# A routed expert chosen from 24 of 32 slots: 19 weight buffers, slot sums in two tiles, the expert's load moved

## The chip, the core and the metric

The kernel runs on one core of a Trainium2 chip. The metric is the device time of one execution in microseconds (us); runs are given as a median with the lowest and highest. The engines are TensorE (PE; PEld is its weight load), VectorE (DVE), ScalarE (ACT), GpSimd (POOL) and SyncE (SP, whose queue issues nearly all transfers here).

## The reference

Three parts follow each other: attention with a bias from relative positions, a soft mixture of experts with 8 experts of 4 slots, and a routed layer in which each token goes to one of 8 experts.

```python
# attention -> x [2304, 512]
logits = x @ phi                                  # [2304, 32 slots]
d = softmax over tokens of logits;  slot_input = d.T @ x
for e in range(8):                                # 4 slots per expert
    h = np.maximum(slot_input[e] @ w1[e], 0.0)    # w1[e] [512, 1024]
    slot_out[e] = h @ w2[e]                       # w2[e] [1024, 512]
c = softmax over slots of logits
x = c @ slot_out
# routed layer
do_compute = x @ w_skip > 0
e_idx = argmax(x @ w_gate)                        # one of 8 experts per token
h = np.maximum(x[mask] @ gw1[e], 0.0)
out = x + gate_w * (h @ gw2[e])                   # tokens without do_compute: out = x
```

## The kernel before

Attention takes the first 340 us. Then come the slots' experts. Their weights, 32 MB, are streamed in 64 pieces of 512 KB: pieces 0 to 31 are the first matrices (four per expert), pieces 32 to 63 the second. `weight_piece` (L228) takes the next buffer and issues the load on SP. The list `SLOTS` (L220) holds 3 + 10 + NW2 buffers: three that are used once, ten that the attention has left (sq, sk, k, bias), and NW2 = 12 new ones (`x0` to `x11`), 25 in all. From piece 25 on a piece reuses the buffer of the piece 22 before it, and its load waits for that piece's matmuls; the last 22 buffers form the ring. The loops over pieces issue one more load after each piece's matmuls.

The first loop (L895 to L902) multiplies pieces 0 to 31 with the slot inputs into `ph`; the second (L975 to L983) multiplies pieces 32 to 63 with the hidden values `hT` into the PSUM tile `pbig`. Between them stand a softmax over slots and its transposes (L909, L869; VectorE's scaling of it is L932), and the transposes of the hidden values (L950). The last piece is loaded in two halves (L243).

After the second loop `pbig` is copied by halves (L985, L986), summed over four row groups with a matmul against `sel` (L989), copied to `ST4` (the 32 slot outputs, transposed; L992, L993) and multiplied with the gate and skip vectors (L996, `pw`), which gives `SW`, the scores of each slot (L1000, L1001). The expert for the routed layer is guessed: a matmul with ones (L1099) sums the scores over the 32 slots, `max` and `max_index` (L1100, L1101) and a clamp (L1102) give an index, SP loads it into a register (L1103) and issues the expert's 4 MB as eight loads of 512 KB (`expert_load`, L1019: four of `w1e`, four of `w2e`). The two tiles lie in the pool `gw`, in memory that the weight buffers had.

Behind that, TensorE runs 19 routing matmuls (L1114), four transposes of `ST4` (L1117), then `slots(0)` with the first quarter of `w1e` (L1034), a counting matmul (L1127) that needs VectorE's `cnt` (L1123), `slots(1)`, `slots_sum(0)` (L1042), and so on in an order written out by hand. `x2` (L1056) forms the output of the slot layer. The list of experts that tokens really chose is compared with the guess (L1219 to L1221): if there is one and it is the guess, a short branch (L1266 to L1283) finishes and stores; otherwise the general branch (L1284) loads each chosen expert again and runs all its matmuls, 24 of 512 columns for each of 18 token tiles.

The order of instructions on each engine comes from a planner that simulates the program, except inside `manual_schedule`, where the order of the source holds: the attention follows the due times of `SCHED` and `LAST`, and everything from L1000 to the stores follows the source. `issue_after(ins)` ties instructions behind one of the same engine. In the two weight loops and between them the planner orders.

```python
def weight_piece():
    i = len(wq)
    name, shape, dt = SLOTS[i] if i < len(SLOTS) else SLOTS[NW + (i - NW) % (len(SLOTS) - NW)]
...
for i in range(32):
    ...
    pe.matmul(po[g * 32:(g + 1) * 32, :], lhsT=hT[:, o:o + NSL], rhs=wq[32 + i][:, a * 512:(a + 1) * 512], start=(i < 2), stop=(i >= 30))
    if len(wq) < 64:
        weight_piece()
...
pe.matmul(pe_g[:, 0:10], lhsT=onesr, rhs=SW, start=True, stop=True)
vec.max(out=g8, in_=pe_g[:, 0:8])
vec.max_index(out=g8i, in_max=g8, in_values=pe_g[:, 0:8])
expert_load(sync.value_load(g_i[0:1, 0:1], min_val=0, max_val=7))
```

Of the kernel before, what the change touches and what calls it, by code (L numbers as in the profile page):

```python
# [9 lines left out]
F32 = mybir.dt.float32  # L10
# [10 lines left out]
P = 128  # L21
# [75 lines left out]
NW2 = 12  # L97
# [8 lines left out]
def soft_moe_attention_kernel(ctx, tc, q, k, v, w1, b1, w2, phi, mw1, mw2,  # L106
# [111 lines left out]
    wq = []  # L218
# [9 lines left out]
    def weight_piece():  # L228
# [593 lines left out]

    for i in range(NW2):
        wpools[f"x{i}"] = wctx.enter_context(tc.tile_pool(name=f"wx{i}", bufs=1, side="right", reuse_waits="tile"))
# [31 lines left out]
    with ExitStack() as mctx:  # L856
# [106 lines left out]
        onesr = late.tile([P, P], F32R, name="onesr")  # L963
# [6 lines left out]
        vec.tensor_copy(onesr, ones)  # L970
# [13 lines left out]
        part = late.tile([P, DM], F32, name="part")  # L984
        act.copy(part[:, 0:256], po[:, 0:256])  # L985
        vec.tensor_copy(part[:, 256:512], po[:, 256:512])  # L986
        pt = [ps.tile([P, 512], F32, name="pc") for _ in range(2)]
        for kc in range(4):
            pe.matmul(pt[kc // 2][:, kc % 2 * P:(kc % 2 + 1) * P], lhsT=part[:, kc * P:(kc + 1) * P], rhs=sel,  # L989
                      start=True, stop=True)  # L990
# [20 lines left out]
    w1e = gw.tile([P, 4, FF], F32, name="w1e")  # L1011
    w2e = gw.tile([P, 8, DM], F32, name="w2e")
# [5 lines left out]

    def expert_load(ereg):  # L1019
        for a in range(4):  # L1020
            f = slice(a * 256, (a + 1) * 256)
            sync.dma_start(out=w1e[:, :, f], in_=gw1[bass.ds(ereg, 1), :, f].rearrange("o (k p) f -> p (o k) f", p=P))
        for a in range(4):
            f = slice(a * 256, (a + 1) * 256)
            sync.dma_start(out=w2e[:, 2 * a:2 * a + 2, :],
                           in_=gw2[bass.ds(ereg, 1), f, :].rearrange("o (k p) f -> p (o k) f", p=P))
# [33 lines left out]
    with tc.tile_pool(name="gq", bufs=1, reuse_waits="tile") as gq:  # L1060
# [33 lines left out]
        g8 = gq.tile([P, 8], F32, name="g8")  # L1094
        g8i = gq.tile([P, 8], mybir.dt.uint32, name="g8i")
# [5 lines left out]
        vec.max_index(out=g8i, in_max=g8, in_values=pe_g[:, 0:8])  # L1101
        vec.tensor_scalar(out=g_i, in0=g8i[:, 0:1], scalar1=7.0, scalar2=0.0, op0=ALU.min, op1=ALU.max)  # L1102
        expert_load(sync.value_load(g_i[0:1, 0:1], min_val=0, max_val=7))  # L1103
        vec.tensor_scalar(out=goff[:, 0:1], in0=g_i, scalar1=8.0, scalar2=None, op0=ALU.subtract)
        vec.tensor_scalar(out=goff[:, 1:2], in0=g_i, scalar1=float(FF), scalar2=None, op0=ALU.mult)
# [10 lines left out]
        for kc in range(4):  # L1116
            pe.transpose(p4[:, kc * P:(kc + 1) * P], ST4[:, kc, :], ident)  # L1117
# [261 lines left out]
```

## Time and profile before

| | us |
|---|---|
| median of 3 runs | 492.16 |
| lowest, highest | 491.25, 494.73 |
| the profiled execution | 491.48 |
| span of its profile | 489.6 |
| PE, DVE, ACT busy | 420.0, 354.4, 301.7 |

The profile shows one execution. Times in its rows count from the start of the span. Busy shares of the whole span mix stages with different limits, so the stretch around the change is read by itself.

### The profile page before, as it was taken

The page shows a single profiled execution, that of the slowest core. Times are in us where ns is not written, and L with a number is a line of the kernel's source. Part 1 is how long each engine was busy: PE and PEld are TensorE (multiplying, and loading weights), DVE is VectorE, ACT ScalarE, POOL GpSimd, SP SyncE. Part 2 cuts the span into 40 slices and gives each one's busy share as a digit, 9 for nine tenths or more (in the row PEclk, how much of TensorE's full clock was granted, in tenths as well). Part 3 has the DMA queues.
Part 4 walks back from the last instruction along what each step waited for, and adds up shares of the span by engine and source line. Part 5 has one row for each costly group of instructions (what it writes and reads, how often), then busy time and mean ns, then how long its engine had stood idle before and what let it go on. Part 6 is the DMA issues. An engine that isn't in the chain of part 4 may idle for free.

```text
span 489.6 us, 11571 instructions
## 1 busy us (share of the span) xinstructions
PE 420.0 (86%) x4291; PEld 302.8 (62%) x4291; DVE 354.4 (72%) x824; ACT 301.7 (62%) x633; POOL 252.6 (52%) x243
## 2 busy tenths in 40 slices
PE   4786997988998989889988999998797777799983
PEld 2442466877888879879967988886363111255462
DVE  6998977976978989878988898996648100047563
ACT  4887978796886888859968879892402100027510
POOL 5630027998887899869997899772300000000000
PEclk9989998998998999989999999999989799959998
DMA  6458864999899999899999989799999999572065
GB/s 184 163 173 306 296 245 88 219 196 234 176 206 210 198 231 187 205 231 197 228 201 245 213 198 175 172 194 215 410 386 407 387 387 387 197 253 93 27 214 177
DMA packets 154076, 111.49 MB, mean 228 GB/s; under 512 B 120256, under 2 KB 126912, under 8 KB 154016
## 3 DMA queue, kind: packets, MB, share of 16 engines
q1 hardware_dynamic: 152112, 107.47, 84.8%
q10 hardware_dynamic: 1824, 2.97, 1.8%
q8 instruction: 36, 0.59, 0.5%
q0 software_dynamic: 80, 0.26, 0.2%
q14 instruction: 24, 0.20, 0.1%
HBM read 66.97 MB, written 15.34 MB: 168 GB/s over the span
## 4 chain that ended last, share of the span: by engine, by line
PE 33%; DMA 33%; DVE 16%; ACT 8%; issue 5%; POOL 3%; SPq 1%; ACTq 0%; DVEq 0%; POOLq 0%
DMA eT<-ehl 9%; PE sc L452 7%; DVE ehl L491 7%; DMA x<-in_moe_w_dram 7%; DMA bias<-in_moe_w_dram 4%; DMA scratch<-ev 4%; DVE e L469 3%; ACT ev L211 3%; PE av L589 3%; PE av L581 2%; PE sc L208 2%; PE ph L899 2%; DMA tn<-in_v_dram 2%; DMA k<-in_moe_w_dram 2%; DMA bias<-scratch 2%
## 5 line engine op out<-in xcount | busy, mean ns | idle before, releaser
L469 DVE CUSTOM_DVE_ANT_0 e<-sc,bias 128x576 f32<-128x576 f32 x128 | 95.0, 753 | 26.9 <-PE sc L452 21.2
L452 PE MATMUL sc<-k,qT 128*128 128x288 f32 x512 | 100.6, 324 | 6.0 <-DVE st L469 4.5
L476 ACT ACTIVATE e<-e,st 128x576 f32<-128x576 f32 x128 | 96.3, 778 | 4.2 <-DVE st L469 3.6
L491 DVE SCALAR_TENSOR_TENSOR ehl<-e,ehl 128x1152 f16<-128x1152 f32 x48 | 83.8, 1746 | 0.5 <-POOL ehl L487 0.4
L452 PEld LDWEIGHTS sc<-k,qT 128*128 128x128 f32 x512 | 74.8, 195 | 11.5 <-DVE st L469 7.4
L487 POOL TENSOR_SCALAR ehl<-e 128x1152 f16<-128x1152 f32 x48 | 60.2, 1262 | 7.9 <-ACT e L476 4.5
L208 PE MATMUL sc<-hid,w2b 128*32 128x288 f32 x576 | 49.9, 433 | 10.7 <-ACT ev L211 7.8
L204 DVE TENSOR_SCALAR hid<-ll,nib 128x576 f32<-128x576 f32 x117 | 55.7, 557 | 2.8 <-PE sc L208 2.8
L395 POOL TENSOR_TENSOR v<-tv,v 128x650 f16<-128x650 f32 x16 | 31.0, 1936 | 44.6 <-ACT v L391 44.6
L424 POOL TENSOR_SCALAR k<-k 64x1152 fp32r<-64x1152 f32 x30 | 51.5, 1717 | 4.6 <-ACT k L414 1.4
L581 PE MATMUL av<-v,eT 128*128 128x65 f16 x1152 | 51.3, 195 | 0.0
L208 PEld LDWEIGHTS sc<-hid,w2b 128*32 128x32 f32 x576 | 23.2, 114 | 35.2 <-ACT ev L211 20.7
L581 PEld LDWEIGHTS <-eT 128*128 128x128 f16 x1152 | 43.8, 99 | 0.9
L1106 POOL TENSOR_SCALAR Lt<-rk 128x128 f16<-128x128 f32 x1 | 0.3, 299 | 75.9 <-PE pbig L980 75.9
L211 ACT ACTIVATE ev<-sc,offs,ipi 128x576 f32<-128x576 f32 x36 | 29.9, 829 | 9.2 <-PE sc L208 5.6
L986 DVE COPY part<-pbig 128x256 f32<-128x256 f32 x1 | 0.4, 425 | 41.7 <-ACT part L985 41.7
L589 PE MATMUL av<-eq,tv 128*64 128x192 f32 x320 | 29.5, 331 | 0.0
L374 POOL TENSOR_SCALAR sk<-tk 128x576 fp32r<-128x576 f32 x16 | 18.1, 1131 | 21.8 <-DMA tk<-in_k_dram 14.5
L376 POOL TENSOR_TENSOR sq<-tq,sq 128x576 fp32r<-128x576 f32 x16 | 27.0, 1690 | 1.1
L985 ACT COPY part<-pbig 128x256 f32<-128x256 f32 x1 | 0.4, 373 | 42.6 <-PE pbig L980 42.6
L544 PE MATMUL pt<-ident,e 128*128 128x128 f32 x144 | 24.8, 285 | 0.5 <-ACT eq L549 0.5
L980 PE MATMUL pbig<-x,hT 128*32 128x512 f32 x76 | 20.5, 623 | 4.8 <-DMA x<-in_moe_w_dram 4.8
(335 smaller groups left out, 881.2 us busy)
## 6 DMA issues: line engine op xcount, KB each, us to landing
x<-in_moe_w_dram SPq DMA_DIRECT2D x30, 512.0 KB, 10.7
scratch<-ev SPq DMA_DIRECT2D x36, 288.0 KB, 4.6
bias<-scratch SPq DMA_DIRECT2D x16, 576.0 KB, 4.7
tn<-in_v_dram SPq DMA_DIRECT2D x32, 224.0 KB, 3.8
bias<-in_moe_w_dram SPq DMA_DIRECT2D x13, 512.0 KB, 10.2
k<-in_moe_w_dram SPq DMA_DIRECT2D x12, 512.0 KB
tk<-in_k_dram SPq DMA_DIRECT2D x16, 288.0 KB, 3.9
tq<-in_q_dram SPq DMA_DIRECT2D x16, 288.0 KB, 4.1
```

The source lines that it names most:

```text
L204: vec.tensor_scalar(out=hid, in0=src, scalar1=nib[:, gi:gi + 1], scalar2=None, op0=ALU.max)
L208: pe.matmul(pb[c * 32:(c + 1) * 32, hh, 0:288], lhsT=w2b, rhs=hid[:, hh * 288:(hh + 1) * 288], start=True, stop=True)
L211: act.activation(ev, pb[:, :, 0:288].rearrange("p a (l u) -> p u a l", u=NU), AF.Identity, bias=offs[not on_act], scale=ipi[:, bt:bt + 1])
L395: pool.tensor_tensor(out=z["v16"][:, 1], in0=tv, in1=z["v16"][:, 0], op=ALU.subtract)
L424: pool.tensor_scalar(out=k1[64 * i:64 * i + 64], in0=k0[64 - 64 * i:128 - 64 * i], scalar1=1.0, scalar2=1.0, op0=ALU.mult, op1=ALU.mult)
L452: pe.matmul(sc[:, hh, 0:288], lhsT=l_, rhs=kf[i][:, o:o + 288], start=(i == 0), stop=(i == 1))
L469: vec.tensor_tensor_reduce(out=z["e", t][:, o].rearrange("p (a j) -> p a j", a=2), in0=z.pop(("sc", t, j))[:, :, 0:288], in1=bias_t[hp, t] ...
L476: act.activation(ee, ee, AF.Exp, bias=z["m", t][:, j:j + 1], scale=-1.0, **kw)
L487: pool.tensor_scalar(out=eh[:, 0], in0=z["e", t], scalar1=ES, scalar2=1.0, op0=ALU.mult, op1=ALU.mult)
L491: vec.scalar_tensor_tensor(out=eh[:, 1], in0=z.pop(("e", t)), scalar=ES, in1=eh[:, 0], op0=ALU.mult, op1=ALU.subtract)
L581: pe.matmul(av[:, oj:oj + VD], lhsT=eT[:, ei, 5 * j + c], rhs=v16[:, vi, c, j], start=False, stop=lastt and k_ == 2 and c == 3)
L589: pe.matmul(z["av", 1][j * 64:(j + 1) * 64, o], lhsT=tv[:, c, j, 0:64], rhs=z["eq"][:, 4 * j + c if c < 4 else 8], start=False, stop=last ...
```

## The change

The ring of weight buffers shrinks (NW2 from 12 to 6: 19 buffers, the last 16 form the ring). The expert's tiles `w1e` and `w2e` get a pool of their own that is open before the weight loops. The second loop writes slots 0 to 23 (pieces 32 to 55) and slots 24 to 31 (pieces 56 to 63) into two PSUM tiles. After piece 55 the first tile is copied, summed over all its rows with ones, multiplied with the gate, and the index of the greatest score becomes the guess; the expert's loads are tied behind the last weight piece on SP. The first tile's part of the slot sums (`to_T(0)`) is done there too, the second tile's after the loop. The guess after `SW` goes, and the four transposes of `ST4` stand ahead of the 19 routing matmuls.

```diff
-NW2 = 12
+NW2 = 6
...
-                eng.dma_start(out=t2[:, a], in_=src[:, a])
+                last_piece[:] = [eng.dma_start(out=t2[:, a], in_=src[:, a])]
...
+    ew = ctx.enter_context(tc.tile_pool(name="ew", bufs=1, side="right", reuse_waits="tile"))
+    w1e = ew.tile([P, 4, FF], F32, name="w1e")
+    w2e = ew.tile([P, 8, DM], F32, name="w2e")
...
-        vec.tensor_copy(onesr, ones)
...
-        po = p1.tile([P, DM], F32, name="pbig", bufs=2)
+        po = [p1.tile([P, DM], F32, name="pbig", bufs=2) for _ in range(2)]
+        part = [late.tile([P, DM], F32, name=f"part{i}") for i in range(2)]
+        pt = [ps.tile([P, 512], F32, name="pc") for _ in range(2)]
+        GE = 24
+        def half_sums(i):
+            act.copy(part[i][:, 0:256], po[i][:, 0:256])
+            vec.tensor_copy(part[i][:, 256:512], po[i][:, 256:512])
+        def to_T(i):
+            for kc in range(4):
+                pe.matmul(pt[kc // 2][:, kc % 2 * P:(kc % 2 + 1) * P], lhsT=part[i][:, kc * P:(kc + 1) * P], rhs=sel,
+                          start=i == 0 and kc % 2 == 0, stop=i == 1 and kc % 2 == 1)
+        def guess_a():
+            half_sums(0)
+            pgs = p1.tile([P, 512], F32, name="pgs")
+            for kc in range(4):
+                pe.matmul(pgs[:, kc * P:(kc + 1) * P], lhsT=part[0][:, kc * P:(kc + 1) * P], rhs=ones,
+                          start=True, stop=True)
+            gsum = sp.tile([P, 512], F32, name="gsum")
+            act.copy(gsum[:, 0:256], pgs[:, 0:256])
+            vec.tensor_copy(gsum[:, 256:512], pgs[:, 256:512])
+            pe_g = p1.tile([P, 10], F32, name="pwg")
+            for kc in range(4):
+                pe.matmul(pe_g, lhsT=gsum[:, kc * P:(kc + 1) * P], rhs=w10[:, kc, :], start=kc == 0, stop=kc == 3)
+            vec.max(out=g8, in_=pe_g[:, 0:8])
+            vec.max_index(out=g8i, in_max=g8, in_values=pe_g[:, 0:8])
+            vec.tensor_scalar(out=g_i, in0=g8i[:, 0:1], scalar1=7.0, scalar2=0.0, op0=ALU.min, op1=ALU.max)
+            with tc.issue_after(last_piece[0].ins):
+                expert_load(sync.value_load(g_i[0:1, 0:1], min_val=0, max_val=7))
...
+            to_T(0)
...
-                pe.matmul(po[g * 32:(g + 1) * 32, :], lhsT=hT[:, o:o + NSL],
-                          rhs=wq[32 + i][:, a * 512:(a + 1) * 512], start=(i < 2), stop=(i >= 30))
+                pe.matmul(po[i // GE][g * 32:(g + 1) * 32, :], lhsT=hT[:, o:o + NSL],
+                          rhs=wq[32 + i][:, a * 512:(a + 1) * 512], start=i % GE < 2, stop=i in (GE - 2, GE - 1, 30, 31))
             if len(wq) < 64:
                 weight_piece()
+            if i == GE - 1:
+                guess_a()
+        half_sums(1)
+        to_T(1)
...
-        pe_g = pg.tile([P, 512], F32, name="pc")
-        pe.matmul(pe_g[:, 0:10], lhsT=onesr, rhs=SW, start=True, stop=True)
-        vec.max(out=g8, in_=pe_g[:, 0:8])
...
-        expert_load(sync.value_load(g_i[0:1, 0:1], min_val=0, max_val=7))
...
+        p4 = pg.tile([P, 512], F32, name="pc")
+        for kc in range(4):
+            pe.transpose(p4[:, kc * P:(kc + 1) * P], ST4[:, kc, :], ident)
         pl = py.tile([P, 512], F32, name="y")[:, 0:NA * 10].rearrange("p (t x) -> p t x", x=10)
         for t in range(NA):
             pe.matmul(pl[:, t, :], lhsT=cT(t) if t < NT else cO, rhs=SW, start=True, stop=True)
-        p4 = pg.tile([P, 512], F32, name="pc")
-        for kc in range(4):
-            pe.transpose(p4[:, kc * P:(kc + 1) * P], ST4[:, kc, :], ident)
```

## Rows read from the trace of the kernel before

**Rows 1.** The page: DMA's busy share in 40 slices, in tenths.
```profile
DMA  6458864999899999899999989799999999572065
```
**Rows 2.** The chain that ended last, 410 us on: start, us, what.
```profile
411.80 10.75 DMA x<-in_moe_w_dram
422.59 2.36 PE pbig L980 x8
...
431.03 4.84 DMA w1e<-in_moe_w_dram
436.00 1.08 PE pc L1034 x8
...
449.96 1.00 PE y L1207 x8
```
**Rows 3.** Timeline, 428 to 437: start, us, engine, line, operation, [idle before <- releaser].
```profile
428.45 1.85 PE L1114 MATMUL y<-SW,bias 128*128 128x10 f32 x8
...
432.29 0.35 PE L1114 MATMUL y<-SW,cO 128*128 128x10 f32 x1
...
432.50 1.11 PE L1117 MATMUL pc<-ident,bias 128*128 128x128 f32 x4
...
433.73 0.42 DVE L1123 TENSOR_REDUCE cnt<-ea 128x8 f32<-128x144 f32 x1
433.92 0.20 PEld L1034 LDWEIGHTS pc<-w1e,bias 128*32 128x32 f32 x8 [0.70 <-DMA w1e<-in_moe_w_dram]
...
434.93 0.60 PE L1127 MATMUL y<-cnt,ones 128*128 128x8 f32 x2
...
436.00 1.08 PE L1034 MATMUL pc<-w1e,bias 128*32 128x256 f32 x8 [0.47 <-DMA w1e<-in_moe_w_dram]
```
**Rows 4.** Stretches: length, five engines' busy us (instructions), granted clock, DMA share, GB/s.
```profile
428.00:429.00 1.00, 0.69 (x4) 0.72 (x4) 0.50 (x4) 0.00 (x0) 0.00 (x0) 0.69 0.00 0
...
431.00:432.00 1.00, 1.00 (x6) 1.00 (x6) 0.00 (x0) 0.00 (x0) 0.00 (x0) 0.50 0.27 52
...
441.00:442.00 1.00, 1.00 (x9) 0.23 (x2) 0.55 (x1) 0.23 (x2) 0.00 (x0) 0.50 1.07 393
442.00:443.00 1.00, 1.00 (x4) 0.56 (x4) 0.59 (x1) 0.49 (x2) 0.00 (x0) 0.98 1.04 383
```
**Rows 5.** Timeline of TensorE in the second weight loop.
```profile
386.90 1.54 PE L980 MATMUL pbig<-x,hT 128*32 128x512 f32 x6
...
413.13 1.05 PE L980 MATMUL pbig<-k,hT 128*32 128x512 f32 x4 [0.30 <-DMA k<-in_moe_w_dram]
```
**Rows 6.** Timeline, 424 to 431: the guess's operations where they stand before.
```profile
424.97 0.37 ACT L985 COPY part<-pbig 128x256 f32<-128x256 f32 x1 [42.64 <-PE pbig L980]
...
425.40 1.17 PE L989 MATMUL pc<-sel,part 128*128 128x128 f32 x8 [0.46 <-ACT part L985]
...
426.63 0.98 PEld L996 LDWEIGHTS pw<-w,bias 128*128 128x128 f32 x8 [0.25 <-issue]
...
429.12 0.15 DVE L1102 TENSOR_SCALAR g_i<-g8i 128x1 int32<-128x1 uint32 x1
...
430.40 2.20 SPq L1022 DMA_DIRECT2D w1e<-in_moe_w_dram  x4
```
**Rows 7.** Timeline, 352 to 365 (first weight loop), and SP's waits, 318 to 436.
```profile
352.04 9.69 SPq L239 DMA_DIRECT2D x<-in_moe_w_dram  x10
...
360.36 0.60 PE L899 MATMUL ph<-sq,sT 128*32 128x256 f32 x8
...
362.61 1.29 DVE L932 TENSOR_TENSOR cn<-ln,cm 128x512 f32<-128x512 f32 x2
362.73 0.33 SPq L239 DMA_DIRECT2D sq<-in_moe_w_dram  x1
...
364.01 0.33 SPq L239 DMA_DIRECT2D sk<-in_moe_w_dram  x1
...
SPq L239 <- DMA x<-in_moe_w_dram: 8.4, 10, 1.0
```

More of the change, by code (lines that the diff above doesn't have):

```diff
@@ L215, in bias_batch @@
                 in_=ev.rearrange("p u a l -> p (u a l)"))
-    wq = []
+    wq, last_piece = [], []
     SLOTS = ([(f"bias{i}", [P, 2 * S], F32) for i in (4,)] + [("w", [P, 1024], F32)] * 2
@@ L821, in soft_moe_attention_kernel, with expert_load @@
     late = ctx.enter_context(tc.tile_pool(name="late", bufs=1, side="right", reuse_waits="tile"))
+    ew = ctx.enter_context(tc.tile_pool(name="ew", bufs=1, side="right", reuse_waits="tile"))
+    w1e = ew.tile([P, 4, FF], F32, name="w1e")
+    w2e = ew.tile([P, 8, DM], F32, name="w2e")
+    def expert_load(ereg):
+        for a in range(4):
+            f = slice(a * 256, (a + 1) * 256)
+            sync.dma_start(out=w1e[:, :, f], in_=gw1[bass.ds(ereg, 1), :, f].rearrange("o (k p) f -> p (o k) f", p=P))
+        for a in range(4):
+            f = slice(a * 256, (a + 1) * 256)
+            sync.dma_start(out=w2e[:, 2 * a:2 * a + 2, :],
+                           in_=gw2[bass.ds(ereg, 1), f, :].rearrange("o (k p) f -> p (o k) f", p=P))
     for i in range(NW2):
@@ L962, in soft_moe_attention_kernel @@
         ones = late.tile([P, P], F32, name="ones")
-        onesr = late.tile([P, P], F32R, name="onesr")
+        g8 = late.tile([P, 8], F32, name="g8")
+        g8i = late.tile([P, 8], mybir.dt.uint32, name="g8i")
         io = late.tile([P, 2, 8], F32, name="io")
@@ L973, in soft_moe_attention_kernel @@
             pool.memset(io[:, 1, e:e + 1], 8.0 - float(e))
-        po = p1.tile([P, DM], F32, name="pbig", bufs=2)
+        po = [p1.tile([P, DM], F32, name="pbig", bufs=2) for _ in range(2)]
[26 more added lines that the diff above has]
+                expert_load(sync.value_load(g_i[0:1, 0:1], min_val=0, max_val=7))
+            vec.tensor_scalar(out=goff[:, 0:1], in0=g_i, scalar1=8.0, scalar2=None, op0=ALU.subtract)
+            vec.tensor_scalar(out=goff[:, 1:2], in0=g_i, scalar1=float(FF), scalar2=None, op0=ALU.mult)
+            to_T(0)
         for i in range(32):
@@ L979, in soft_moe_attention_kernel @@
                 o, g = f * 256 + e * NSL, f % 4
-                pe.matmul(po[g * 32:(g + 1) * 32, :], lhsT=hT[:, o:o + NSL],
-                          rhs=wq[32 + i][:, a * 512:(a + 1) * 512], start=(i < 2), stop=(i >= 30))
+                pe.matmul(po[i // GE][g * 32:(g + 1) * 32, :], lhsT=hT[:, o:o + NSL],
+                          rhs=wq[32 + i][:, a * 512:(a + 1) * 512], start=i % GE < 2, stop=i in (GE - 2, GE - 1, 30, 31))
             if len(wq) < 64:
                 weight_piece()
[L984 to L987, printed above, removed]
-        for kc in range(4):
-            pe.matmul(pt[kc // 2][:, kc % 2 * P:(kc % 2 + 1) * P], lhsT=part[:, kc * P:(kc + 1) * P], rhs=sel,
-                      start=True, stop=True)
+            if i == GE - 1:
+                guess_a()
+        half_sums(1)
+        to_T(1)
         st4 = ST4.rearrange("p k s -> p (k s)")
@@ L1009, in soft_moe_attention_kernel @@
     py = ctx.enter_context(tc.tile_pool(name="py", bufs=4, space=PSUM, reuse_waits="tile"))
-    w1e = gw.tile([P, 4, FF], F32, name="w1e")
-    w2e = gw.tile([P, 8, DM], F32, name="w2e")
     w2h = gw.tile([P, 8, DM], F32R, name="w2h")
@@ L1017, in soft_moe_attention_kernel @@
     G = gw.tile([P, FF], F32R, name="G")
[L1019 to L1026, printed above, removed]
     gs = {}
@@ L1114, in soft_moe_attention_kernel @@
             pe.matmul(pl[:, t, :], lhsT=cT(t) if t < NT else cO, rhs=SW, start=True, stop=True)
-        p4 = pg.tile([P, 512], F32, name="pc")
-        for kc in range(4):
-            pe.transpose(p4[:, kc * P:(kc + 1) * P], ST4[:, kc, :], ident)
         l8 = pl[:, :, 0:8]
```

6 lines of the change are left out of this document (removed).

## The prediction

> **What bounds the kernel now.** I read the 40 slices first, then the chain of work that ended last from 410 us on, then the timeline of that stretch engine by engine, then the stretch table for clock and DMA share. The strip of slices (12.24 us each) shows DMA at 9 up to 416 us and 5, 7, 2 after that [rows 1]: the stage that multiplies the 64 weight pieces is paced by transfers. The chain agrees: eight pieces in 10.75 us, 1.34 us each, then the last matmuls at 422.59 [rows 2]. The reader should then see the hole: matmuls end at 422.59 + 2.36 = 424.95, the chain comes back to DMA only with the expert's weights at 431.03, and goes on with the slot matmuls at 436.00 [rows 2]. That looks like five or six microseconds of waiting for one transfer. It is not, and this decides the forecast. In the hole TensorE works: 19 routing matmuls from 428.45 to 432.64, four transposes from 432.50, and only then slots(0) at 433.92, whose weight load had waited 0.70 us for w1e; slots(1) at 436.00 waited 0.47 us [rows 3]. All that time the clock is at 1.2 GHz: it falls in the stretch 428 to 429 (0.69 on average) and is back to 2.4 GHz in 442 to 443 (0.98) [rows 4]. So in the hole the chain names a transfer, but TensorE stands right behind it.
>
> **The change part by part.**
>
> *The early load.* Piece 55 is the last that the first 24 slots need. Its matmuls start at 413.13 [rows 5], last 1.05, end at 414.18. Copies of the two halves (0.37 for the first [rows 6], as much again for the second) bring us to about 415.0; eight passes as in L989 (1.17 [rows 6]), two copies (0.8), eight passes as in L996 (0.98 of weight loads [rows 6]) to about 418.0; then max, index and clamp, some 0.7. In the old order the clamp ended at 429.12 + 0.15 and SP issued at 430.40 [rows 6], 1.13 later; the same step puts the new issue at about 419.8. The last piece lands near 424, so w1e follows with no gap: 4 MB at 1.34 us per 0.5 MB is in by about 435, the first quarter by 425.5. TensorE asks for it at 432.6 (below), so this part could come 7 us later at no cost. The register load blocks SP until 418.7, but all weight pieces are ahead of it and behind it stand only the expert's eight loads and, much later, the stores.
>
> *What the tail gains.* SW, pw, the copies before them and the 19 routing matmuls stay. The guess matmul of L1099 goes and the four transposes move ahead of the routing matmuls, into the wait for SW (pw's weight loads end at 426.63 + 0.98 = 427.61 [rows 6], the routing matmuls began at 428.45). At 2.4 GHz the transposes take about half of their 1.11 us [rows 3], so the routing matmuls start and end as before, at 432.64. slots(0) then starts at 432.6 instead of 433.92: 1.3 earlier. The counting matmul still needs cnt: VectorE ends cnt at 433.73 + 0.42 = 434.15 [rows 3], 1.5 us after the last routing matmul, and that stays; so it runs at 434.15 to 434.75 (0.60 [rows 3]) and slots(1) starts at 434.75 instead of 436.00: **1.25 us gained**. What is late next is TensorE itself: from 436 on slots, sums and bounds follow each other with no transfer between, and w2e is first used at 449.96 [rows 2]. Bounds: 0.47 (only the wait at slots(1) goes) to 1.4 at the same clock.
>
> *What TensorE pays before 425.* The guess adds 8 + 8 passes, and the sums in two tiles 8 more. At 0.123 us a pass (0.98 / 8 [rows 6]) that is 2.95 us. Cover: a piece's four passes take 1.05 when alone, but that has the drain in it; six in a row took 1.54, 0.257 each [rows 5], so a piece needs at most 1.03 and leaves 0.3 us of its 1.34, by the rows' face value 2.4 us over eight pieces. Taking off one drain per piece (1.05 to about 0.87, from six passes in 1.54 with one drain) the gap is 0.47 and the cover 3.8 us. By the first reading the last matmul ends 0.6 us later, and up to 1.7 later if TensorE also stands still for the copies; by the second it ends on time, save for one wait that isn't made up. I take 0.2, nearer the second, since back-to-back passes are what a backlog gives; ends 0 and 1.7. The copies lie on ACT and VectorE, idle there.
>
> The row shows weight loads at 0.98 of the 1.04 us of L996, so they set a pass of few columns [rows 6]. The Trainium skill (TensorE: Matmul & The Clock Gate, Step-by-step) says that the array can take a weight load ahead of a matmul in flight; by it a guess pass behind a 512-column pass would hide its load, and the sum would have 0 here instead of 0.2.
>
> *19 buffers instead of 25.* Piece 19 now takes the buffer of piece 3 and waits for its matmuls; before, this wait began at piece 25. SP issued pieces 15 to 24 from 352.04, and 25 at 362.73, 26 at 364.01, one per landing, since eight are in flight (the waits of SP for transfers say so) [rows 7]; so 17 landed at 362.7 and 18 at 364.0. Now 16 to 18 are in flight when piece 3's matmuls, 360.36 + 0.60 [rows 7], free the buffer at 361.0. From issue to first bytes I take 1.3 us (issue at 430.40 [rows 6]; DMA share 0.27 in 431 to 432 [rows 4]): bytes at 362.4, 1.6 before the queue runs dry. Cost 0, bounds 0 and, if an eighth of the stream's depth mattered, 1 us. Later, pieces 32 to 47 can be issued as soon as the first 32 are used, and eight in flight never need more; cost 0.
>
> For that first-byte time the Trainium skill (DMA: Bandwidth & Descriptors, Specifications) states some 0.6 us for this path. The row has twice that and decides; by the page the margin would be 2.3 us.
>
> *The rest.* One cast (onesr) goes, two small tiles move; VectorE is idle there: 0.
>
> *Sum.* -1.25 + 0.2 = -1.05 on the profiled execution of 491.48 (span 489.6 and 1.9 around it): 490.4. That execution lies 0.7 below the median of 492.16; on the median it would be 491.1. I give **490.8**.
>
> **The rivals.**
>
> *A. The clock comes back earlier.* For: 13 us at 1.2 GHz [rows 4], in which a routing matmul takes 1.85 / 8 = 0.23 [rows 3] where a pass of L996 takes 0.12 [rows 6], and dense work now begins 1.25 us sooner with no wait between slots(0) and slots(1). Against: what precedes the fall (short passes, gaps) stays nearly the same. If the clock rose near 437 instead of 442, TensorE's six busy us there would shrink to four, the copies of ACT then binding: -2; if it did not fall at all, the routing matmuls save 19 x 0.1 = 1.9 more. 486.5 to 488.5; I take 488.
>
> *B. The guess is not hidden.* Its passes and waits stand in the stream: 1.7 lost against 1.25 gained, 491.9, on the median 492.6: no change.
>
> *C. The weight stream runs dry* (slower). The place is piece 19 behind piece 3's matmuls. If TensorE's new order puts the first routing transposes ahead of piece 3, they wait for L932, whose first half ends at 362.61 + 0.65 = 363.3 [rows 7]; with 0.8 of transposes and 0.6 of matmuls the buffer is free at 364.7, bytes come at 366.1, 2.1 after the queue is dry. Transfers pace all up to 425, so all of it arrives: 491.48 - 1.05 + 2.1 = 492.5, on the median 493.2; each further microsecond one more. It decides from a release at 363.7 on, 2.7 later than now. Against: before, TensorE did the first 20 pieces in one go.
>
> *D. The change doesn't do what it says.* Either the register load stands ahead of weight pieces on SP (pieces 56 on are then issued at 418.7, eight pieces of 1.34 land at 430.8 instead of 424: +7), or the guess misses: then the general branch runs 18 x 24 passes of 0.257 [rows 5], over 90 us more. Against: the load is tied behind the last piece. From the reference's formulas and inputs, the gate scores summed over 24 slots are 0.0123 for expert 0 and 0.0040 for the next, over 32 slots 0.0095 and 0.0019: the same expert, and all tokens go to it.
>
> **How the numbers follow.** Forecast 0.58 (own range 489.3 to 492.3), A 0.12, B 0.12, C 0.12, D 0.06. From 487.3 to 494.3 the range takes in the forecast, B, most of C, and half of A. About 1% (4.9 us) is what a measurement here can tell from no change. Faster by more needs A in full: 0.08. Slower by more needs D or a long C: 0.07. Within: 0.85.
>
> **What would show it.** Right: SP issues w1e near 420, DMA stays full to about 435, and slots(0) starts some 7.6 us after the last weight matmul instead of 9.0; no wait for w1e is left in that stretch, and the span falls by one, not by five. Wrong: slots(0) follows the last weight matmul sooner than 6.5 us, or the clock is at 2.4 GHz before 438 (A); matmuls of the last pieces follow each other without waiting and end past 426 (B); DMA share below 0.9 between 360 and 370 (C); no DMA between 414 and 418 (D).

## The result and the profile after

The changed kernel took 490.99 us (median of 20 runs, 486.60 to 499.43). The kernel before, run beside it, took 495.38 us (20 runs, 491.25 to 497.38). The ratio is 0.9911, with a 95% interval of 0.9883 to 0.9939: between 3.0 and 5.8 us were gained, 4.4 in the middle. The ratios, here and below, are formed from those runs of each kernel that lie within 1.5% of its fastest, the medians from all its runs, so a ratio can differ from the quotient of the medians beside it (492.20 to 496.87 below is 0.9906, where 0.9859 stands). The forecast of 490.8 us lies 0.2 from the measured median, but that is luck and no proof of its working: two of the three runs of the kernel before that the forecast started from (median 492.16) turned out to be the fastest of its twenty. The forecast gain was 1.05 us, the measured one about four times that, and the profile shows where most of it arose.

Much of the spread between the profiled executions comes from the attention. The load of weight piece 3 (the first into `sq`; "start" below) is issued at 338.6 us in the profile before, at 339.5 in the one after, and anywhere up to 350.3 in the profiles further down. It stands ahead of the stage that the change is about; whether the change moves it is open. So profiles are compared here by two lengths: the **stream**, from that issue to ScalarE's copy that follows the last weight matmul, and the **tail**, from there to the end of the span.

| us | before | after | difference |
|---|---|---|---|
| profiled execution, span | 491.48, 489.6 | 489.07, 487.3 | -2.3 of span |
| start of the stream | 338.60 | 339.53 | +0.93 (attention) |
| stream | 86.37 | 87.73 | **+1.36** |
| tail up to the start of slots(1) | 11.03 | 8.19 | **-2.84** |
| tail from there on | 53.60 | 51.85 | **-1.75** |

Without the attention's share that is -3.2 us, at the near end of the measured interval; what makes the rest up to 4.4 is not shown. The forecast had +0.2, -1.25 and 0 in the last three rows.

The page of the changed kernel: its span, the granted clock and DMA's busy share in 40 slices of 12.18 us.

```profile
span 487.3 us, 11616 instructions
...
PEclk9987998999998999999989999999978999979998
DMA  6558782999999999999999999799999999890066
```

Where the strip before had 5, 7, 2 from 416 us on [rows 1] it now has 8, 9, 0 from 414 on: the expert's weights follow the last weight piece nearly at once and are all there by 440.

The chain of the changed kernel that ended last, from 414 us on (start, us, what).

```profile
414.44 10.45 DMA x<-in_moe_w_dram
424.94 2.30 PE pbig L1027 x8
...
430.50 2.89 PE y L1140 x19
433.42 0.32 DVE mx L1142
...
434.93 0.60 PE y L1150 x2
435.52 1.01 PE pc L1067 x8
```

The transfer of `w1e` that stood in the chain before [rows 2] is gone; behind the last weight matmul the chain runs through TensorE, one copy on ScalarE and VectorE's counting.

The timeline of the changed kernel in the first weight loop and around the end of the second (start, us, engine, line, operation, [idle before <- releaser]). L912 is the first loop, L1027 the second, L1005 and L1012 the guess, L998 the slot sums, L1137 the transposes, L1140 the routing matmuls, L1067 slots, L1150 the counting matmul.

```profile
361.73 1.08 PE L912 MATMUL ph<-sq,sT 128*32 128x256 f32 x8
...
417.30 0.71 PE L1005 MATMUL pgs<-ones,part 128*128 128x128 f32 x4 [0.47 <-ACT part L993]
...
422.30 1.06 PE L1012 MATMUL pwg<-w,gsum 128*128 128x10 f32 x8
...
424.94 2.29 PE L1027 MATMUL pbig<-x,hT 128*32 128x512 f32 x8 [0.18 <-DMA x<-in_moe_w_dram]
425.17 2.50 SPq L830 DMA_DIRECT2D w1e<-in_moe_w_dram  x4
...
429.84 0.64 PE L1137 MATMUL pc<-ident,bias 128*128 128x128 f32 x4
...
430.50 1.05 PE L1140 MATMUL y<-SW,bias 128*128 128x10 f32 x8
...
431.42 1.75 PE L1140 MATMUL y<-SW,w 128*128 128x10 f32 x10
...
433.02 0.35 PE L1140 MATMUL y<-SW,cO 128*128 128x10 f32 x1
...
433.31 1.08 PE L1067 MATMUL pc<-w1e,bias 128*32 128x256 f32 x8
...
434.93 0.60 PE L1150 MATMUL y<-cnt,ones 128*128 128x8 f32 x2 [0.54 <-DVE cnt L1146]
...
435.45 1.08 PE L1067 MATMUL pc<-w1e,bias 128*32 128x256 f32 x8
```

The first eight routing matmuls take 1.05 us where they took 1.85 [rows 3], all nineteen 2.87 (430.50 to 433.37) where they took 4.19. slots(0) starts 6.05 us after the last weight matmul instead of 8.95, slots(1) 8.19 instead of 11.03, and neither waits for `w1e`.

Stretches of the changed kernel, of 1 us: length, five engines' busy us (instructions), granted clock, DMA share, GB/s.

```profile
362.00:363.00 1.00, 1.00 (x12) 0.39 (x8) 0.55 (x1) 0.41 (x1) 0.00 (x0) 0.50 0.74 303
363.00:364.00 1.00, 1.00 (x16) 0.52 (x12) 0.90 (x4) 0.00 (x0) 0.00 (x0) 0.63 0.26 74
...
366.00:367.00 1.00, 1.00 (x24) 0.57 (x20) 0.00 (x0) 0.00 (x0) 0.00 (x0) 1.00 0.75 242
...
425.00:426.00 1.00, 1.00 (x5) 0.21 (x6) 0.00 (x0) 0.00 (x0) 0.00 (x0) 1.00 0.08 31
...
431.00:432.00 1.00, 1.00 (x11) 1.00 (x11) 0.00 (x0) 0.09 (x1) 0.00 (x0) 1.00 1.07 379
432.00:433.00 1.00, 1.00 (x7) 1.00 (x7) 0.00 (x0) 0.00 (x0) 0.00 (x0) 0.50 1.08 376
...
439.00:440.00 1.00, 1.00 (x11) 0.36 (x10) 0.31 (x1) 0.73 (x3) 0.40 (x1) 1.00 0.06 23
```

The clock falls to 1.2 GHz only at 432, and is back at 2.4 GHz in 439 to 440; before, it was low from 428 to 442 [rows 4]. The other news is in 362 to 364: the weight stream has a hole where it had none (share at or above 0.99 in every microsecond from 352 to 384 of the profile before).

### The profile page after: what moved, and what is told of

The parts are those of the page before. It is cut to its first block, busy times and chain, and to the rows that moved or that the text cites. A ratio compares the mean times of both kernels' runs of the same rounds, so it can differ in the third digit from the quotient of the medians.

```text
span 487.3 us, 11616 instructions
## 1 busy us (share of the span) xinstructions
PE 421.2 (86%) x4314; PEld 306.5 (63%) x4314; DVE 353.6 (73%) x825; ACT 301.8 (62%) x635; POOL 252.8 (52%) x243
## 4 chain that ended last, share of the span: by engine, by line
PE 33%; DMA 33%; DVE 14%; ACT 8%; issue 6%; POOL 3%; SPq 1%; ACTq 0%; DVEq 0%; POOLq 0%
DMA eT<-ehl 9%; DMA k<-in_moe_w_dram 8%; PE sc L452 7%; DVE ehl L491 7%; DMA x<-in_moe_w_dram 6%; PE sc L208 4%; DMA scratch<-ev 4%; PE av L581 3%; ACT ev L211 2%; DVE e L469 2%; PE av L589 2%; DVE xnat L1303 2%; PE pt L544 1%; POOL ehl L487 1%; PE pt L407 1%
## 5 line engine op out<-in xcount | busy, mean ns | idle before, releaser
L491 DVE SCALAR_TENSOR_TENSOR ehl<-e,ehl 128x1152 f16<-128x1152 f32 x48 | 81.7, 1702 | 1.2 <-POOL ehl L487 1.1
L208 PE MATMUL sc<-hid,w2b 128*32 128x288 f32 x576 | 51.8, 457 | 10.8 <-ACT ev L211 7.7
L424 POOL TENSOR_SCALAR k<-k 64x1152 fp32r<-64x1152 f32 x30 | 52.5, 1749 | 4.2 <-ACT k L414 1.3
L374 POOL TENSOR_SCALAR sk<-tk 128x576 fp32r<-128x576 f32 x16 | 18.1, 1134 | 21.2 <-DMA tk<-in_k_dram 14.4
L589 PEld LDWEIGHTS av<-eq,tv 128*64 128x64 f32 x320 | 21.6, 136 | 4.7 <-issue 2.0
L577 PE MATMUL av<-v,eT 128*128 128x130 f16 x144 | 16.8, 227 | 8.1 <-DMA eT<-ehl 8.1
```

The source lines that it names most:

```text
L208: pe.matmul(pb[c * 32:(c + 1) * 32, hh, 0:288], lhsT=w2b, rhs=hid[:, hh * 288:(hh + 1) * 288], start=True, stop=True)
L424: pool.tensor_scalar(out=k1[64 * i:64 * i + 64], in0=k0[64 - 64 * i:128 - 64 * i], scalar1=1.0, scalar2=1.0, op0=ALU.mult, op1=ALU.mult)
L491: vec.scalar_tensor_tensor(out=eh[:, 1], in0=z.pop(("e", t)), scalar=ES, in1=eh[:, 0], op0=ALU.mult, op1=ALU.subtract)
L589: pe.matmul(z["av", 1][j * 64:(j + 1) * 64, o], lhsT=tv[:, c, j, 0:64], rhs=z["eq"][:, 4 * j + c if c < 4 else 8], start=False, stop=last ...
```

## The experiments

All of them compute the whole output. Each was timed beside the kernel before on the same chip. "25, 23, 19 buffers" are the weight buffers; the lengths in the table are read from each one's profile as above. "To w2e" is the first part of "from slots(1)", up to the first matmul with `w2e`. "Low" is how long the clock stays at 1.2 GHz behind the start of slots(1) until it comes back for the first time. Not counted in it are the last 2.5 to 4.5 us of the span, at 1.2 GHz in all fourteen profiles, and 3.4 us from 455.8 on in the second profile of the kernel before.

| kernel | ratio to before (95%) | stream | to slots(1) | from slots(1) | to w2e | low |
|---|---|---|---|---|---|---|
| before | | 86.37 | 11.03 | 53.60 | 13.89 | 6.0 |
| before, once more | | 86.88 | 11.21 | 55.03 | 14.40 | 7.6 |
| changed | 0.9911 (0.9883 to 0.9939) | 87.73 | 8.19 | 51.85 | 12.99 | 3.4 |
| changed, once more | 0.9908 (0.9867 to 0.9949) | 88.16 | 8.38 | 53.45 | 14.07 | 6.4 |
| before, new order only | 1.0007 (0.9973 to 1.0042) | 86.82 | 11.11 | 53.13 | 13.79 | 5.8 |
| changed, loads late | 1.0006 (0.9966 to 1.0045) | 88.13 | 10.33 | 52.08 | 13.08 | 3.6 |
| changed, old order | 0.9966 (0.9927 to 1.0005) | 87.22 | 9.83 | 52.18 | 13.24 | 3.9 |
| before, wide | 0.9990 (0.9957 to 1.0023) | 87.28 | 10.89 | 54.86 | 15.75 | 8.0 |
| changed, wide | 0.9859 (0.9808 to 0.9910) | 88.32 | 7.45 | 51.30 | 11.78 | 0 |
| before, 19 buffers only | 1.0020 (0.9977 to 1.0064) | 90.01 | 11.29 | 53.36 | 13.66 | 5.5 |
| changed, 23 buffers | 0.9899 (0.9842 to 0.9955) | 86.49 | 7.77 | 53.14 | 13.42 | 4.3 |
| the same, other buffer order | 0.9884 (0.9834 to 0.9934) | 86.73 | 7.60 | 52.73 | 13.59 | 4.6 |
| 23 buffers, wide | 0.9849 (0.9803 to 0.9896) | 87.19 | 7.44 | 51.22 | 11.84 | 0 |
| the same, other buffer order | 0.9893 (0.9835 to 0.9952) | 86.40 | 7.45 | 51.33 | 11.81 | 0 |

**The kernel before, once more.** Not edited; a second profile, to see what one profile is worth.

> The kernel before once more, for a second profile. If the split of the gain is right (stream 1 to 2 us longer, tail some 4 us shorter in the changed kernel), this one has 86.3 to 87.3 us from the first load of the stream to the last weight matmul, no dip in the first weight loop, and 64 to 66 us from there to the end with 10 to 14 us at 1.2 GHz. If the first profile of before was an odd one, the tail is below 62.5.

One execution, 498.28 us. Its timeline, TensorE around the routing matmuls:

```profile
433.60 1.03 PE L1114 MATMUL y<-SW,bias 128*128 128x10 f32 x8
...
436.12 1.11 PE L1117 MATMUL pc<-ident,bias 128*128 128x128 f32 x4
...
439.26 1.08 PE L1034 MATMUL pc<-w1e,bias 128*32 128x256 f32 x8 [2.03 <-DMA w1e<-in_moe_w_dram]
```

Here the same program began its routing matmuls at 2.4 GHz (1.03 us for eight), and slots(0) came no sooner for it: 9.10 us after the last weight matmul, with 2.03 us of waiting for `w1e` in place of the matmuls' extra time. The clock of one stretch can differ between executions of one program. The tail is 66.24 us, 1.6 longer than in the first profile and a little above what was expected; 1.59 of that lies where the clock is low a second time, from 455.8 to 459.2.

**The changed kernel, once more**, in a later group of runs.

> The changed kernel once more, for a second profile and on one chip with the next two. Both theories: 87.2 to 90 us from the first load of the stream to the last weight matmul, with a dip of DMA's share in the first weight loop; 59.5 to 61.5 us from there to the end; ratio to before 0.988 to 0.994.

The ratio repeats (0.9908). The tail of 61.83 is a little above the expected 61.5: the clock stayed low for 6.4 us behind slots(1), as long as in the kernel before. Stream 88.16 and tail 61.83 give, with the first profile, means of 87.9 and 60.9, against 86.6 and 65.4 for the two profiles before: +1.3 and -4.5.

**The new order alone** (kernel before; the load stays where it was):

```diff
+        p4 = pg.tile([P, 512], F32, name="pc")
+        for kc in range(4):
+            pe.transpose(p4[:, kc * P:(kc + 1) * P], ST4[:, kc, :], ident)
...
         for t in range(NA):
             pe.matmul(pl[:, t, :], lhsT=cT(t) if t < NT else cO, rhs=SW, start=True, stop=True)
-        p4 = pg.tile([P, 512], F32, name="pc")
-        for kc in range(4):
-            pe.transpose(p4[:, kc * P:(kc + 1) * P], ST4[:, kc, :], ident)
```

> The kernel before with the four transposes of ST4 ahead of the guess matmul and the routing matmuls; buffers and the late load stay. Theory load (the wait for w1e is what the tail pays): slots(0) still starts when w1e lands, 9 us after the last weight matmul, gain under 0.4 us. Theory clock (the holes in TensorE's work let the clock fall, and filling one keeps it at 2.4 GHz longer): the fall comes after 430 instead of 428.6 and the run is 0.5 to 2 us faster.

495.70 us, ratio 1.0007. Its timeline:

```profile
431.24 1.03 PE L1117 MATMUL y<-SW,bias 128*128 128x10 f32 x8
...
433.18 2.20 SPq L1022 DMA_DIRECT2D w1e<-in_moe_w_dram  x4
433.25 0.25 PE L1117 MATMUL y<-SW,cO 128*128 128x10 f32 x1
...
436.69 1.08 PE L1034 MATMUL pc<-w1e,bias 128*32 128x256 f32 x8 [3.19 <-DMA w1e<-in_moe_w_dram]
```

TensorE is through with the routing at 433.5, all of it at 2.4 GHz, and then stands still for 3.19 us. The time saved on TensorE turns into waiting for `w1e`: slots(0) starts 8.83 us after the last weight matmul, 8.95 before. The clock fell later, at 434.5, as theory clock had it, but the time is what theory load expected.

**The changed kernel with late loads** (the new order stays; the index reaches SP only after `SW`):

```diff
-            with tc.issue_after(last_piece[0].ins):
-                expert_load(sync.value_load(g_i[0:1, 0:1], min_val=0, max_val=7))
...
+        vec.scalar_tensor_tensor(out=g_i, in0=SW[:, 0:1].bitcast(F32), scalar=0.0, in1=g_0, op0=ALU.mult, op1=ALU.add)
+        expert_load(sync.value_load(g_i[0:1, 0:1], min_val=0, max_val=7))
```

> The changed kernel with the expert's index passed on only after SW is there, so that the loads are issued as late as before, about 5.5 us behind the last weight matmul; all else as changed. Theory load: the gain of the early transfer goes, slots(0) waits for w1e again, and the run is 1.2 to 4 us slower than the changed one (ratio to before 0.994 to 0.999). Theory clock: the routing matmuls still run at 2.4 GHz up to 432, slots(0) waits for w1e and the clock is lost in that wait; half of the gain stays (0.993 to 0.996).

496.78 us, ratio 1.0006: the whole gain is gone, more of it than either theory expected. Its timeline:

```profile
437.11 2.50 SPq L830 DMA_DIRECT2D w1e<-in_moe_w_dram  x4
...
440.75 1.08 PE L1068 MATMUL pc<-w1e,bias 128*32 128x256 f32 x8 [2.63 <-DMA w1e<-in_moe_w_dram]
```

The wait for `w1e` is back. The loads are issued 4.52 us behind the last weight matmul (5.43 in the kernel before). The tail of this profile is still 2.2 us shorter than in the kernel before, but its stream with 19 buffers is 1.76 longer, so that 0.5 us is left.

**The changed kernel with the old order** (the loads early, the four transposes back behind the routing matmuls; the diff is that of the new order, backwards).

> The changed kernel with the four transposes of ST4 back behind the 19 routing matmuls; the early load stays. With the runs order (transposes moved alone: no gain) and late (load late again: no gain) in hand, theory both: the two waits end at the same time, so each part alone gains nothing and only both together do; then this run stands near before, ratio 0.996 to 1.000, with the clock down at 1.2 GHz during the routing matmuls. Theory load: the early transfer alone gains, ratio 0.990 to 0.994.

496.40 us, ratio 0.9966, not told apart from no change. Its timeline:

```profile
438.23 1.70 PE L1137 MATMUL y<-SW,bias 128*128 128x10 f32 x8 [0.61 <-DVE SW L1045]
...
442.13 1.11 PE L1140 MATMUL pc<-ident,bias 128*128 128x128 f32 x4
443.18 1.08 PE L1067 MATMUL pc<-w1e,bias 128*32 128x256 f32 x8
```

No wait for `w1e`, but the routing matmuls are at 1.2 GHz again and the transposes stand behind them at the same clock. slots(0) starts 8.29 us after the last weight matmul, 0.66 sooner than before, and slots(1) 1.20 sooner; that is what the early load was worth by itself (with the guess's matmul gone from this stretch). The stream of this profile is 0.85 us longer than before's, and takes back a part.

The three together: at slots(0) the early load alone gains 0.66 us, the new order alone 0.1, both 2.9; at slots(1) 1.20, nothing (11.11 against 11.03) and 2.84. Two chains ran side by side behind the last weight matmul, TensorE's own and the expert's load, and ended within a microsecond of each other.

**Wide routing matmuls.** If the clock is what is left, routing matmuls that give the array more columns might keep it up. `SW` gets 118 columns of zeros, the next token tile's matmul overwrites their place (excerpt):

```diff
+WD = 128
...
-    SW = const.tile([P, 10], F32R, name="SW")
+    SWw = const.tile([P, WD], F32R, name="SWw")
+    SW = SWw[:, 0:10]
...
+    pool.memset(SWw.bitcast(F32), 0.0)
...
-            pe.matmul(pl[:, t, :], lhsT=cT(t) if t < NT else cO, rhs=SW, start=True, stop=True)
+            pe.matmul(plw[:, t * 10:t * 10 + WD], lhsT=cT(t) if t < NT else cO, rhs=SWw, start=True, stop=True)
```

(In the changed kernel `T4t` also shares `S4t`'s tile, to make room.) The changed kernel first:

> The changed kernel with the 19 routing matmuls 128 columns wide instead of 10 (118 columns of zeros, each overwritten by the next), so that TensorE streams columns under its weight loads. Theory clock: the clock stays at 2.4 GHz through the slot matmuls, the six microseconds at 1.2 GHz from 432 on go, and the run is 1 to 2.5 us faster than the changed one (ratio to before 0.985 to 0.990). Theory load: nothing moves, 0.991.

492.20 us against 496.87, ratio 0.9859. Its timeline:

```profile
434.60 1.11 PE L1144 MATMUL y<-SWw,bias 128*128 128x128 f32 x8
...
436.87 0.64 PE L1070 MATMUL pc<-w1e,bias 128*32 128x256 f32 x8
...
438.48 0.39 PE L1154 MATMUL y<-cnt,ones 128*128 128x8 f32 x2 [0.97 <-DVE cnt L1150]
```

And one stretch of it, from the slot sums on:

```profile
431.00:444.00 13.00, 10.87 (x84) 7.04 (x83) 7.27 (x27) 5.16 (x15) 0.84 (x5) 1.00 0.90 317
```

Thirteen times the columns cost next to nothing (1.11 us for eight instead of 1.05), the clock stays at 2.4 GHz throughout this stretch, and slots(0) takes 0.64 us instead of 1.08. What is late next is VectorE: the counting matmul now waits 0.97 us for `cnt`.

The same in the kernel before:

> The kernel before with wide routing matmuls alone. Theory clock: its gain needs no early load: the clock stays up through the slot matmuls, 1 to 2.5 us faster, ratio 0.995 to 0.998. Theory both: TensorE is through with the routing matmuls sooner but then waits for w1e, 9 us behind the last weight matmul as before, and loses the clock there: ratio 0.999 to 1.001.

495.80 us, ratio 0.9990. Its timeline:

```profile
433.40 1.07 PE L1121 MATMUL pc<-ident,bias 128*128 128x128 f32 x4
...
436.56 1.08 PE L1037 MATMUL pc<-w1e,bias 128*32 128x256 f32 x8 [2.09 <-DMA w1e<-in_moe_w_dram]
```

And the stretch in which its clock falls:

```profile
432.50:433.00 0.50, 0.50 (x7) 0.50 (x5) 0.00 (x0) 0.00 (x0) 0.00 (x0) 0.84 0.00 0
```

TensorE is ready sooner and waits 2.09 us for `w1e`, as theory both expected. But the clock was not lost in that wait: it fell at 432.8, while the wide routing matmuls ran and TensorE was busy all the time, and the four transposes ahead of the wait already take 1.07 us instead of the 0.64 at 2.4 GHz. That is 5.3 us after the last weight matmul, against 5.1 in the second profile of the kernel before. So wide matmuls do not keep the clock up by themselves. The three profiles whose clock does not fall here have them together with the new order and the early load; which of the two they need was not tried.

**The weight buffers.** The smaller ring alone, in the kernel before:

```diff
-NW2 = 12
+NW2 = 6
```

> The kernel before with NW2 = 6 and nothing else. Theory ring (in the changed kernel's profile DMA's share fell to 0.26 to 0.76 between 362 and 368 us, because piece 19 waits for piece 3): the same dip stands here, and the run is 1.0 to 2.5 us slower than before (ratio 1.002 to 1.005). Theory harmless (what the prediction held: the buffer comes free 1.6 us before the stream runs dry): no dip, ratio 1.000 within 0.002.

498.15 us, ratio 1.0020: in the time no difference. In its profile there is one, in stretches of 1 us:

```profile
364.00:365.00 1.00, 1.00 (x16) 0.41 (x10) 0.79 (x2) 0.15 (x1) 0.00 (x0) 0.50 0.59 238
365.00:366.00 1.00, 1.00 (x16) 0.45 (x12) 0.43 (x1) 0.54 (x1) 0.00 (x0) 0.53 0.08 33
366.00:367.00 1.00, 1.00 (x24) 0.55 (x20) 0.90 (x4) 0.00 (x0) 0.00 (x0) 1.00 0.00 0
```

The stream stands still for two microseconds and is 90.01 us long, 2.7 to 3.6 more than in the four profiles with 25 buffers. One profile against timings that would hide up to 3 us (0.64% of 497): the hole is shown, its price in the median is not.

Then 23 buffers in the changed kernel: only `w1e` gets early memory, `w2e` goes back to the pool `gw` and is loaded after `SW` (excerpt):

```diff
-NW2 = 6
+NW2 = 10
...
-    w2e = ew.tile([P, 8, DM], F32, name="w2e")
...
+    w2e = gw.tile([P, 8, DM], F32, name="w2e")
...
+        expert_load2(regs[0])
```

> The changed kernel with only w1e in the early pool, w2e back in the later pool (its loads follow w1e's once the weight buffers are free) and NW2 = 10, 23 buffers. Theory ring: DMA's dip in the first weight loop goes, from the first load of the stream to the last weight matmul it takes 86.3 to 86.9 us instead of 87.7 to 90.0, and the run is 1 to 3 us faster than the changed one (ratio to before 0.984 to 0.989); w2e lands before its use at some 20 us behind the last weight matmul, so the late half of the load costs nothing. Theory harmless: no change against the changed kernel, 0.991.

494.58 us against 497.47, ratio 0.9899, with a stream of 86.49 as expected, but hardly faster than the changed kernel. With the wide routing matmuls:

> Both: 23 buffers with w2e late, and routing matmuls 128 columns wide. If the two gains stand in different stretches they add: 86.3 to 86.9 us of stream and under 59.5 us from the last weight matmul to the end, ratio to before 0.978 to 0.985.

489.65 us, ratio 0.9849; the tail of 58.66 us is as expected, the stream of 87.19 is not. The hole did not go: summed over the microseconds from 352 to 384, the DMA share is short of 1 by 1.1 us in the profile of 23 buffers and by 1.8 in this one, where the five changed kernels with 19 buffers have 1.3 to 2.6. It has another reason: SP's load into the fourth of the ten new buffers waits for the end of the attention. Two buffers that I took to lie over the attention's tile `e` went to the end of the list:

```diff
-             + [(f"x{i}", [P, 1024], F32) for i in range(NW2)])
+             + [(f"x{i}", [P, 1024], F32) for i in (0, 1, 2, 5, 6, 7, 8, 9, 3, 4)])
```

> The run ring23 with its new buffers used in the order 0, 1, 2, 5 to 9, 3, 4: in ring23 the load into x3 stood on SP for 4 to 5 us, because that memory held the attention's tile e until the slot sums had read it. Theory ring: a load that waits for its buffer is what makes the dip, so it goes now (under 0.3 us of missing share between 352 and 384), the stream takes 86.2 to 86.9 us, and the run is 0.8 to 3 us faster than the changed kernel on the same chip. Theory noise: the dips cost nothing that arrives, no difference.

491.43 us, ratio 0.9884, beside 0.9908 for the changed kernel on the same chip: not told apart. SP's waits in it, 340 to 375 us (line, waited for: us in total, times, longest):

```profile
SPq L239 <- DVE e L763: 4.3, 1, 4.3
...
SPq L239 <- PE pt L770: 1.8, 1, 1.8
```

The wait is still there (4.1 us in the first run with 23 buffers), and 1.1 us of share are missing where under 0.3 were expected. In both profiles it follows the first three loads into the new buffers, whatever names stand there, so it may be that memory is given out in the order of the list, and that the edit left the places as they were; no run shows it. With the wide matmuls too:

> The run ring23b with the 19 routing matmuls 128 columns wide. If both gains hold: 86.2 to 86.9 us of stream, 58.3 to 59.3 us behind it with no stretch at 1.2 GHz up to the slot matmuls, ratio to before 0.978 to 0.985, and the fastest of all versions.

489.68 us, ratio 0.9893, above the expected 0.978 to 0.985, and no faster than the wide version with the list in its first order (489.65); in its one profile stream and tail are both among the shortest (86.40 and 58.78), as expected.

The streams of all profiles by buffers: 25 buffers 86.37 to 87.28 (four, mean 86.8), 23 buffers 86.40 to 87.19 (four, mean 86.7), 19 buffers with the early load's memory 87.22 to 88.32 (five, mean 87.9). So in the changed kernel the smaller ring costs the stream about 1.1 us, and 23 buffers give it back.

Both best ratios are of wide versions, 0.9849 (23 buffers) and 0.9859 (19). Their intervals overlap that of the change itself (0.9883 to 0.9939), and the repeat with 23 buffers in another order gave 0.9893, so a gain beyond the change is likely by the profiles (tails of 58.7 to 58.8 against 60.0 and 61.8) but not shown by the times.

## Why the prediction was right and where it was wrong

**What the hole hides: right.** TensorE did stand right behind the transfer: either part alone gains 1.20 us or nothing at slots(1), both 2.84.

**The early load: right in what it costs, 5.4 us off in time.** The forecast had SP issue `w1e` at 419.8; it did so at 425.17. Half of that is the stream: piece 55's matmuls start at 415.78 instead of 413.13. For the rest, the planner put the guess's passes between weight pieces (417.30 to 423.36), which I had counted as one block. That left a hole in the transfers (DMA share 0.08 in 425 to 426), and it costs nothing, as the forecast said such a delay would: slots(0) asks at 433.31 and does not wait. The register load held up no weight piece; the last of them was issued before it (rival D did not come).

**The guess's passes: right, at 0 instead of 0.2.** The last eight weight matmuls still wait 0.18 us for their transfer, so TensorE was not late. They end at 427.23, past the 426 that was to show rival B, but because of the stream, not of the guess. The cover in the sum was too large: with 1.05 for four passes and 1.54 for six [rows 5], two passes cost 0.49, four without the drain 0.98 and not 0.87, and the cover over eight pieces is 2.9 us and not 3.8, just the 2.95 that it had to hold.

**The tail: the step that failed is "so the routing matmuls start and end as before, at 432.64".** They start 3.24 us after the last weight matmul instead of 3.48, and end 6.11 after it instead of 7.67, because the first 1.5 us of them run at 2.4 GHz. That is 1.56 us which the sum didn't have. Added to its 1.25 us it makes 2.81, and 2.84 were measured at slots(1). The 1.25 itself, that slots(1) then follows the counting matmul, 1.5 us behind the routing, came as worked out (434.93 is 1.56 behind 433.37). I had reasoned that what precedes the fall "stays nearly the same". It did not: the four transposes now run in the gap between `pw` and the routing matmuls, and in the six profiles that have them there, with routing matmuls of 10 columns, the clock fell 4.5 to 7.1 us after the last weight matmul. With the transposes behind, it fell at 3.1 to 3.5 in three profiles and at 5.1 in one, the repeat of the kernel before. So the order goes with a later fall, but the old order does not always bring an early one.

**The rest of the tail: the forecast's 0 was 1.75, but only 0.90 of it is the clock's.** I let the clock come back where it did before. It came back 3.4 us behind slots(1) instead of 6.0. The first matmul with `w2e` (timeline) and VectorE's last sum, the last line of the chain, show where the time went. The kernel before:

```profile
449.89 1.07 PE L1207 MATMUL y<-w2e,hO 128*32 128x512 f32 x8
...
481.52 0.75 DVE xnat L1280
```

The changed one:

```profile
448.44 1.07 PE L1230 MATMUL y<-w2e,hO 128*32 128x512 f32 x8
...
480.07 0.75 DVE xnat L1303
```

From slots(1) to `w2e` it is 12.99 us instead of 13.89: 0.90 gained. From there to the last sum both take 31.63. From the end of that sum to the end of the span, where the last stores run, it is 6.48 instead of 7.33, and these 0.85 are scatter: over the fourteen profiles that stretch takes 6.5 to 7.3 us whatever the kernel, 6.50 in the second profile of the kernel before and 7.01 in that of the changed one.

What the clock is worth stands in the column to `w2e`: 11.8 us where nothing of it is at 1.2 GHz, rising with the low stretch to 14.4 at 7.6. A straight line through thirteen profiles has 0.35 us for each microsecond at 1.2 GHz, and no point is far from it; left out is the wide kernel before, which waits another 1.64 us for `w1e` there. By it, 2.6 us less make 0.9, the whole of what was measured. It does not come each time: the second profile of the changed kernel is low for 6.4 us and takes 14.07, and over the two profiles of each kernel 0.6 are gained here, against 2.84 up to slots(1). The wide version of the changed kernel is the test of this, since it alters the clock and little else: 3.4 us less at 1.2 GHz, 1.21 us less to `w2e`. All this is rival A, with chance 0.12, and its sign (slots(0) sooner than 6.5 us) was there: 6.05. For the routing matmuls it had 1.9 us if the clock did not fall at all; 1.32 came (2.87 instead of 4.19) with the clock falling half-way through them. For what follows it had 2, and 0.90 came.

**Nineteen buffers: the cost was not 0, but 1.1 to 1.4 us.** Two terms were off, and a third a little. The buffer comes free later: piece 3's matmuls run 361.73 to 362.81, and SP issues piece 19 at 362.87. Set back by the 0.93 us by which the stream starts later, that is 361.9, not 361.0; these matmuls now run at 1.2 GHz (1.08 us where they took 0.60 [rows 7]). And the queue is dry sooner: the share is down to 0.74 already in 362 to 363, so the last transfer in flight ended near 363.0, 362.1 with the same shift, where I had 364.0 from counting eight in flight. That count took SP's next issue for the end of a transfer's bytes; by the bytes moved since the start of the stream (8.95 MB at the hole), the kernel before was as far at about 362.1 too, so the queue itself was no shorter. The third term was too long rather than too short: the 1.3 us from issue to first bytes are 1.05 (last section). The margin of 1.6 us thus became a gap of about 0.9. After that the ring of 16 refills only as fast as TensorE frees it, 0.75 in 366 to 367. The forecast's upper bound for this term was 1 us; measured is a little more. Rival C named this place and the sign to look for, a share below 0.9 between 360 and 370, but its cause was another: VectorE's scaling and the order on TensorE; here it was the clock and a queue that ran dry sooner than counted, at 1.1 to 1.4 of its 2.1 us.

**The sum.** -2.84 - 1.75 + 1.36 = -3.2 us where -1.05 was forecast, and -2.4 of it without the scatter behind the last sum. The likeliest case did not happen; rival A did, with a small C set against it. The median fell close to the forecast by luck, because the runs that it started from were faster than the kernel's later ones, and within 1% is what came, 0.9 in the middle of an interval that reaches 1.2.

## What to carry to other kernels

When the chain names one wait, look at what the other engines do meanwhile and when they would be ready: two chains that end within a microsecond hide each other, each change alone is not told apart from nothing (1.0007, 1.0006, 0.9966; the last two with the longer stream of 19 buffers in them), and only both together pay (0.9911). Where a stretch runs at 1.2 GHz, don't carry that clock over into the forecast as if it belonged to the stretch; an edit that fills a gap ahead of it can move it, and matmuls of few columns can be widened with zeros to try it, at 0.06 us for eight here; it kept the clock up in three versions and did not in a fourth. Before a shorter tail is credited to an edit, look where along the tail it became shorter: half of one gain here lay behind the last computation, where the profiles scatter. Buffers that were "one too many" in a steady stream may have been covering its start: compare the time at which the reused buffer is freed with the time at which the last transfer in flight ends, read from the trace and not from a count.

## What the runs showed that was not expected

A routing matmul of 128 columns took hardly longer than one of 10: eight in 1.11 us against 1.05 at the same clock.

From the issue of `w1e` to its first bytes it is less than the 1.3 us that the forecast read from the kernel before [rows 4, 6]. That figure takes the busy share of a microsecond as if all of it lay at the end of the stretch, and the trace of the new order alone would give the same by it: issued at 433.18, no transfer in the stretch from 433 on, a share of 0.53 in the next.

```profile
433.00:434.00 1.00, 0.50 (x5) 0.41 (x4) 0.46 (x3) 0.00 (x0) 0.00 (x0) 1.00 0.00 0
434.00:435.00 1.00, 0.00 (x0) 0.00 (x0) 0.93 (x4) 0.00 (x0) 0.00 (x0) 0.76 0.53 144
```

In stretches of 0.05 us the first transfer begins 1.05 us after the start of SP's issuing instruction, in these two profiles and in four more with a quiet queue; the instruction itself takes 0.38, so that it is 0.67 from its end. The Trainium skill (DMA: Bandwidth & Descriptors, Specifications) has some 0.6 us for this path. Counted from the end of the issue the traces agree with it; the forecast's "twice that" does not hold.

The rate of the weight stream differs with the use of early memory. Taken over the 13 us that end 13 us before ScalarE's copy, at a full DMA share (1.04 to 1.05), it was 385 to 387 GB/s in the five profiles without the early pool, that with 19 buffers included; 401 to 403 in the five with 19 buffers and both expert tiles early; 391 or 392 in the four with 23 buffers and `w1e` alone. The stretch of the kernel before, then of the changed one:

```profile
398.97:411.97 13.00, 9.98 (x40) 1.44 (x40) 0.00 (x0) 0.00 (x0) 0.00 (x0) 1.00 1.05 387
...
401.26:414.26 13.00, 10.52 (x40) 1.44 (x40) 0.00 (x0) 0.00 (x0) 0.30 (x1) 1.00 1.05 403
```

Four per cent of a 13 us stretch is half a microsecond, so this gave back a part of what the hole cost: the changed kernel's DMA share was short of 1 by 2.0 us in all between 352 and 384, and its stream was only 1.36 longer. That it is the place of the buffers, and of which, was not tried.
